# Attention with an MLP on one TensorE: each product with v split over two row halves, summed in two PSUM banks

## The chip, the core and the metric

One core of one Trainium2 chip runs the whole program. The metric is the device time of one execution in microseconds (us); lower is better.

## What is computed

`g * A(x) + (1 - g) * B(x)` for x of 2048 tokens by 576 features, in float32. A is softmax attention over all 2048 tokens with 32 heads of 18 features, B is a layer norm and an MLP of 4608 hidden units with a tanh GELU, and g a sigmoid gate per token.

```
q, k, v = qkv[0], qkv[1], qkv[2]
scores = jnp.einsum("bhqd,bhkd->bhqk", q, k) * Dh ** -0.5
p = _softmax(scores, axis=-1)
o = jnp.einsum("bhqk,bhkd->bhqd", p, v)
a = o.transpose(0, 2, 1, 3).reshape(B, S, D) @ wo
h = _gelu(jnp.einsum("bsd,df->bsf", layernorm(x), w1) + b1)
b = jnp.einsum("bsf,fd->bsd", h, w2) + b2
return g * a + (1 - g) * b
```

## The kernel before

The program has three stages: projections to q, k and v (to about 245 us of the profiled execution), a long loop in which attention and the MLP share TensorE (to about 2162 us), and the end of the output projection.

**Units.** The heads are taken in 16 pairs, and the queries in two halves of 1024: 32 units. A pair's two heads lie on the two row halves of the array, so a score product has 54 or 56 rows and 128 columns, and two of them run side by side. A unit has 16 steps (`kc`, 128 keys each) of two half steps (`qb`, 512 queries each). In a half step stand:

- `s2` (line 320): two score products, keys by queries. ScalarE takes the exponential of each (line 322) into a ring of buffers `p` and `ring`, which frees its PSUM bank.
- one round of `s1` (line 234): two score products for a later unit, queries by keys, of which VectorE takes the row maxima (line 236), which frees their banks.
- then either a stretch of the MLP (lines 611 and 751, written as pairs of products on the two row halves, `weave`), or of the output projection late in the loop (line 1353), or a visit to `pv`.

**The product with v.** `pv` (line 339) multiplies two or three finished steps (`room`) with v: for each step four products of 128 keys by 32 columns, one for each head and query block, which write partitions 0, 64, 32 and 96 of one bank and run in four column groups of the array. They accumulate over the 16 steps of the unit. The operands are float32 and not float32r as elsewhere, and the profile shows two matmul rows for each such product. At the end of the unit `o_store` copies the bank with VectorE (line 364) and stores it.

**Banks.** PSUM has eight banks. In the loop the MLP has two of its own (`ps_w`). The other six (`ps_x`, class `Earliest`) serve `s1`, `s2` and the open sum of a unit. Which bank a product takes is decided when the program is written: the one that a small model of the engines' clocks (`pe_t`, `act_t`, `dve_t`, `let_go`) believes to be free first. On the chip the product then waits for the engine that read the bank's former tile.

**Order.** The order on each engine is fixed by the code: `run_due` counts slots, and `defer(n, fn)` puts a piece of work n slots later. `s1_finish` turns a unit's maxima into two extra rows of q with such delays: `parts` on ScalarE, then `rows` on VectorE (lines 257 and 258) with eight small stores into `qa`. For unit 0 this lies ahead of the loop, where `looped[0]` is false.

Of the kernel before, what the change touches and what calls it, by code (L numbers as in the profile page):

```python
# [12 lines left out]
ALU = mybir.AluOpType  # L13
# [10 lines left out]
NT = S // P  # L24
# [39 lines left out]
def gated_mix_kernel(ctx: ExitStack, tc: tile.TileContext, x, wqkv, wo, w1, b1, w2, b2, gate_w, out):  # L64
    nc = tc.nc
# [34 lines left out]
    pe_t, act_t, dve_t = [0.0], [0.0], [0.0]  # L100
# [10 lines left out]
    taken = [0]  # L111
    ps_x = Earliest()
# [5 lines left out]
    def let_go(i, clock, ns):  # L118

        clock[0] = max(clock[0], pe_t[0] + DRAIN) + ns  # L120
        free_at[i] = clock[0]
# [5 lines left out]
    def psum(pool):  # L127
        return pool.tile([P, TB], F32, name="ps")
# [10 lines left out]
    def dma_r(queue, dst, src):  # L139

        queue.dma_start(dst.bitcast(F32), src)  # L141
# [5 lines left out]
    def defer(n, fn):  # L147
        later.append((slot[0] + n, fn))
# [13 lines left out]
    def run_due(ns=SLOT):  # L162

        slot[0] += 1
        now[0] += ns
        if chain and chain[0][0]():
            chain.pop(0)[1]()
        due = [f for t, f in timed if t <= now[0]]
        timed[:] = [(t, f) for t, f in timed if t > now[0]]
        for f in due:  # L170
            f()
        due = [f for s, f in later if s <= slot[0]]
        later[:] = [(s, f) for s, f in later if s > slot[0]]
        for f in due:
            f()
        k = 0
        while k < len(bg):
            if pool_end[0] - now[0] < bg[k][2] and slot[0] >= bg[k][0]():
                bg.pop(k)[1]()
                k = 0  # L180
            else:
                k += 1
# [12 lines left out]
    def unit(u):  # L195
        return UNITS[u]
# [44 lines left out]
    def s1_finish(u):  # L241

        m4 = M4.pop(u)
        nm = asm.tile([P, 2, 2, 8], F32, name="nm")
        nm2 = asm.tile([P, 2, 2, 8], F32, name="nm2")
        nmh = asm.tile([P, 2, 8], F32R, name="nmh")
        nc.vector.tensor_reduce(nm[:, 0], m4, axis=AX.X, op=ALU.max, negate=True)

        def parts():
            nc.scalar.activation(nmh, nm[:, 0], AF.Copy)  # L250
            nc.scalar.activation(nm[:, 1], nmh.bitcast(F32), AF.Copy, scale=-1.0)
            nc.scalar.activation(nm2[:, :, 0, :], nmh.bitcast(F32), AF.Copy)
            defer(2 if looped[0] else 8, rows)

        def rows():
            mr = asm.tile([P, 32], F32, name="mr", bufs=1)
            nc.vector.tensor_reduce(nm2[:, :, 1, :], nm.rearrange("p k a b -> p a b k"), axis=AX.X, op=ALU.add)
            nc.vector.transpose(mr, nm2.rearrange("p a b c -> p (a b c)"))
            qa = QA[u % 3]
            aside = slot[0] < ybusy[0]  # L260

            def store(h, k):
                r = 64 * h + 54
                c = 32 * k + 16 * h
                dst = qa[r:r + 2, :].rearrange("b (t k n) -> b t k n", k=4, n=32)[:, :, k, :]
                dma_r(nc.scalar if aside else nc.sync, dst, mr[c:c + 16, :])
            for n in range(8):
                if aside:
                    defer(1 + n, lambda n=n: store(*divmod(n, 4)))
                else:  # L270
                    store(*divmod(n, 4))
        defer(3 if looped[0] else 2, parts)

    RING = []

    def ring(n):
        return RING[n % 4 if n < NARROW else (n - NARROW) % 3]
# [6 lines left out]
    def flush():  # L284

        if held:
            for fn in waiting:
                fn()
            waiting.clear()
            tail = held.pop()  # L290
            tail()
# [45 lines left out]
    OB = {}  # L337

    def pv(n0, n1):

        flush()
        for c in range(n0, n1):
            u, k = divmod(c, NT)
            if k == 0:
                OB[u] = psum(ps_x), taken[0]
            v = VT[UNITS[u][0] % 2]
            for qb in range(2):
                for h in range(2):
                    r = 32 * (2 * h + qb)
                    nc.tensor.matmul(OB[u][0][r:r + 32, :], v[:, k, 19 * h:19 * h + 32], ring(c)[:, qb, h, :],  # L350
                                     start=(k == 0), stop=(k == NT - 1))
            pe_t[0] += 1040.0
            if k == NT - 1:
                o_store(u, *OB.pop(u))
        run_due(1040.0 * (n1 - n0))

    stored = []

    def o_store(u, ps, bank):

        pair, half = unit(u)
        oe = asm.tile([P, TB], F32, name="oe", bufs=1)
        dn = asm.tile([P, 16], F32, name="dn", bufs=1)
        nc.vector.tensor_copy(oe, ps)
        let_go(bank, dve_t, 620.0)
        cols = slice(2 * pair * DH, 2 * (pair + 1) * DH)
        nc.sync.dma_start(dn, oe[DH::32, :])
        for h in range(2):
            for qb in range(2):
                c = 32 * (2 * h + qb)  # L370
                d = (2 * pair + h) * DH
                q = half * HALF + qb * TB
                nc.sync.dma_start(ot_scr[0, d:d + DH, q:q + TB], oe[c:c + DH, :])

        def spread():
            nc.vector.reciprocal(dn, dn)
            nc.sync.dma_start(dn_scr[u], dn)
            defer(16 if u < NU - 3 else 4, wide)

        def wide():  # L380
            dst = ot_scr[1, cols, half * HALF:(half + 1) * HALF]
            nc.sync.dma_start(dst.rearrange("(h d) n -> h d n", d=DH), dn_scr[u][:, None, :].to_broadcast([2, DH, HALF]))
            stored.append(u)
        defer(24 if u < NU - 3 else 4, spread)
# [4 lines left out]
    looped = [False]  # L389
# [511 lines left out]
    with ExitStack() as a:  # L901
# [217 lines left out]
        for tb in range(NB):  # L1119
# [3 lines left out]
            for g, (fn, args) in enumerate(work):  # L1123
# [49 lines left out]
                if tb == 2 and g == 13:  # L1173
                    ps = psum(ps_x)
# [242 lines left out]
    for u in range(NU):  # L1417
        for kc in range(NT):
# [22 lines left out]
            if step - done[0] >= room[0] or room[0] == 3 and ended[0] and step > done[0]:  # L1441
                pv(done[0], step)
                done[0] = step
                piece[0] = 0
                ended[0] = 0
            else:
                fill(step)
            s2(u, kc, 1, loop_round(), 462.0)
            if not (room[0] == 3 and ended[0]):
                fill(step)  # L1450
    pv(done[0], NSTEP)
    while stream or later or timed or chain:
        filler(spent[0] + 1000.0)
# [26 lines left out]
```

## Time and profile before

| | us |
|---|---|
| median of three runs | 2215.01 (2215.0 to 2216.78) |
| profiled execution | 2215.03, of which the span from the first to the last instruction is 2213.1 |
| TensorE (PE) busy | 2196.4 |
| weight loads (PEld) busy | 1599.6 |
| VectorE (DVE) busy | 1644.7 |
| ScalarE (ACT) busy | 1436.3 |
| GpSimd (POOL) busy | 949.1 |
| loop, 260 to 2131 us: PE, DVE, ACT busy | 1869.1, 1448.6, 1312.8 |

The mean granted TensorE clock is 0.998. Matmuls overlap, so the busy time of PE says that something is always in flight, and not how close together products start; the start times in the timeline say that. Idle time of an engine is put down to whatever semaphore came last before it.

### The profile page before, as it was taken

What the parts mean: (1) busy time and instruction counts of PE and PEld (TensorE: products, weight loads), DVE (VectorE), ACT (ScalarE), POOL (GpSimd) and SP (SyncE); (2) the same over time, 40 slices, a digit from 0 to 9 for tenths busy, and PEclk for the clock granted to TensorE, in tenths of its full rate; (3) what the DMA queues carried; (4) which work ended last, traced back from release to release, by engine and by line L of the source; (5) the groups of instructions that cost most, each with busy time, mean ns of one, the idle gap of its engine ahead of it and who ended that gap; (6) DMA issues with size and microseconds to landing.
All of it is one profiled execution on the core that took longest, in us unless ns stands there. A gap on an engine that the chain in (4) does not pass through costs nothing. (4 is left out here: it accounts for less than half of the span.)

```text
span 2213.1 us, 51656 instructions
## 1 busy us (share of the span) xinstructions
PE 2196.4 (99%) x20569; PEld 1599.6 (72%) x20569; DVE 1644.7 (74%) x2887; ACT 1436.3 (65%) x2719; POOL 949.1 (43%) x936
## 2 busy tenths in 40 slices
PE   8999999999999999999999999999999999999999
PEld 7878777777767777677677676776677677777668
DVE  5675777777777777777777777777777777787844
ACT  4223677777776666666666666666766667666771
POOL 4002566666663444444445444444534444444420
PEclk9999999999999999999999999999999999999999
DMA  7755654536485423342273424243563333333355
GB/s 241 259 190 188 206 172 140 171 133 179 152 230 184 127 102 122 101 145 92 104 187 141 125 100 124 101 126 120 137 187 113 135 113 106 116 109 117 97 177 182
DMA packets 163414, 323.65 MB, mean 146 GB/s; under 512 B 59838, under 2 KB 86370, under 8 KB 152338
## 3 DMA queue, kind: packets, MB, share of 16 engines
q1 hardware_dynamic: 159462, 313.60, 44.4%
q10 hardware_dynamic: 3712, 6.75, 0.8%
q8 instruction: 162, 2.65, 0.5%
q14 instruction: 78, 0.64, 0.1%
HBM read 229.07 MB, written 95.16 MB: 147 GB/s over the span
## 5 line engine op out<-in xcount | busy, mean ns | idle before, releaser
L236 DVE TENSOR_REDUCE m<-ps 128x1 f32<-128x512 f32 x2048 | 1307.5, 684 | 392.0 <-PE ps L234 354.9
L322 ACT ACTIVATE p<-ps 128x512 f32<-128x512 f32 x1080 | 582.6, 596 | 283.4 <-PE ps L234 188.8
L322 ACT ACTIVATE ring<-ps 128x512 f32<-128x512 f32 x968 | 523.2, 596 | 259.5 <-PE ps L234 186.5
L320 PE MATMUL ps<-qa,ka 56*128 56x512 f32 x2048 | 685.9, 409 | 4.5 <-DMA qa<-mr 2.6
L234 PE MATMUL ps<-ka,qa 54*128 54x512 f32 x2048 | 625.6, 409 | 0.9 <-DVE big L968 0.7
L611 PE MATMUL ps<-big,w 64*128 64x512 f32 x3888 | 516.5, 392 | 0.1
L320 PEld LDWEIGHTS ps<-qa,ka 56*128 56x128 f32 x2048 | 358.4, 185 | 212.0 <-DVE m L236 130.8
L751 PE MATMUL ps<-w,hh 64*128 64x288 f32 x4352 | 491.2, 293 | 0.9 <-ACT z L636 0.8
L187 POOL TENSOR_SCALAR zz<-zz 128x512 f32<-128x512 f32 x272 | 169.2, 622 | 742.7 <-ACT zz L702 714.1
L751 PEld LDWEIGHTS ps<-w,hh 64*128 64x128 f32 x4352 | 418.1, 186 | 22.1 <-ACT z L636 1.2
L611 PEld LDWEIGHTS ps<-big,w 64*128 64x128 f32 x3888 | 380.6, 185 | 72.2 <-ACT vt L1066 0.3
L187 POOL TENSOR_TENSOR zz<-zz,z 128x512 f32<-128x512 f32 x280 | 361.8, 1293 | 35.9 <-ACT zz L705 9.8
L751 PE MATMUL ps<-w,hl 64*128 64x288 f32 x2176 | 340.7, 293 | 0.0
L234 PEld LDWEIGHTS ps<-ka,qa 54*128 54x128 f32 x2048 | 318.2, 186 | 23.1 <-issue 3.6
L350 PE MATMUL ps<-p,vt 128*32 128x512 f32 x2160 | 265.2, 598 | 0.0
L350 PE MATMUL ps<-ring,vt 128*32 128x512 f32 x1936 | 238.9, 598 | 0.0
L751 PEld LDWEIGHTS ps<-w,hl 64*128 64x128 f32 x2176 | 236.9, 186 | 0.0
L187 POOL TENSOR_TENSOR w<-x,w 128x576 fp32r<-128x576 f32 (+1 forms) x34 | 68.2, 2009 | 271.2 <-ACT w L490 206.6
L187 POOL TENSOR_TENSOR hl<-zz,hh 128x512 fp32r<-128x512 f32 x134 | 174.6, 1304 | 14.0 <-ACT hh L664 3.2
L350 PEld LDWEIGHTS ps<-p,vt 128*32 128x32 f32 x2160 | 57.9, 109 | 126.8 <-issue 124.2
L350 PEld LDWEIGHTS ps<-ring,vt 128*32 128x32 f32 x1936 | 52.3, 109 | 112.2 <-issue 111.2
L1037 PE MATMUL ps<-big,wqk 128*128 128x512 f32 x504 | 123.5, 400 | 0.0
(120 smaller groups left out, 1452.0 us busy)
## 6 DMA issues: line engine op xcount, KB each, us to landing
w<-w_scr SPq DMA_DIRECT2D x54, 1152.0 KB
w<-w_scr SPq DMA_DIRECT2D x108, 576.0 KB
w_scr<-w SPq DMA_DIRECT2D x18, 1152.0 KB
w_scr<-w SPq DMA_DIRECT2D x36, 576.0 KB
qa<-qk_scr SPq DMA_DIRECT2D x192, 72.0 KB
ka<-qk_scr SPq DMA_DIRECT2D x90, 144.0 KB
big<-y_scr SPq DMA_DIRECT2D x48, 256.0 KB
x<-in_B_w_dram SPq DMA_DIRECT2D x34, 288.0 KB
```

The costliest lines, as they stand in the source:

```text
L187: fn(*args, **kw)
L234: nc.tensor.matmul(ps, qa[r0:r0 + 54, t * P:(t + 1) * P], ka[r0:r0 + 54, kb * TB:(kb + 1) * TB], start=True, stop=True)
L236: nc.vector.tensor_reduce(M4[u][:, h, t, kb:kb + 1], ps, axis=AX.X, op=ALU.max)
L320: nc.tensor.matmul(ps, ka[r0:r0 + 56, kc * P:(kc + 1) * P], qa[r0:r0 + 56, qb * TB:(qb + 1) * TB], start=True, stop=True)
L322: nc.scalar.activation(ring(n)[:, qb, h], ps, AF.Exp, scale=SCALE)
L350: nc.tensor.matmul(OB[u][0][r:r + 32, :], v[:, k, 19 * h:19 * h + 32], ring(c)[:, qb, h, :], start=(k == 0), stop=(k == NT - 1))
L611: nc.tensor.matmul(ps[h], wt[w_][r, c, :], Y[s_][r, c, :], start=(k == 0), stop=(k == 26))
L751: mm = nc.tensor.matmul(ps[nn][:, :ND], h_[r, tok], w_[p_][r, cs[nn]], start=(k == 0 or bare and k == 3 * G), stop=(k == 6 * G - 1 or bare ...
L1037: nc.tensor.matmul(ps, w_[:, c, ms], big[:, s_, :], start=(k == 0), stop=(k == len(prods) - 1))
```

## The change

Each product with v is written as two, over keys 0 to 63 and 64 to 127 of the step. The tiles are 64 rows by 32 columns instead of 128 by 32. The upper and the lower half accumulate in two banks, so a unit's open sum holds two banks of the six. At the end of a unit VectorE copies the first bank and adds the second to the copy. One delay ahead of the loop goes from 8 slots to 4.

```diff
-            defer(2 if looped[0] else 8, rows)
+            defer(2 if looped[0] else 4, rows)
...
-                OB[u] = psum(ps_x), taken[0]
+                OB[u] = [(psum(ps_x), taken[0]) for _ in range(2)]
...
                 for h in range(2):
-                    r = 32 * (2 * h + qb)
-                    nc.tensor.matmul(OB[u][0][r:r + 32, :], v[:, k, 19 * h:19 * h + 32], ring(c)[:, qb, h, :],
-                                     start=(k == 0), stop=(k == NT - 1))
+                    for part in range(2):
+                        r = 32 * (2 * h + qb)
+                        keys = slice(64 * part, 64 * part + 64)
+                        nc.tensor.matmul(OB[u][part][0][r:r + 32, :], v[keys, k, 19 * h:19 * h + 32], ring(c)[keys, qb, h, :],
+                                         start=(k == 0), stop=(k == NT - 1))
             pe_t[0] += 1040.0
             if k == NT - 1:
-                o_store(u, *OB.pop(u))
+                o_store(u, OB.pop(u))
...
-    def o_store(u, ps, bank):
+    def o_store(u, parts):
...
-        nc.vector.tensor_copy(oe, ps)
-        let_go(bank, dve_t, 620.0)
+        nc.vector.tensor_copy(oe, parts[0][0])
+        let_go(parts[0][1], dve_t, 620.0)
+        nc.vector.scalar_tensor_tensor(oe, parts[1][0], 1.0, oe, op0=ALU.mult, op1=ALU.add)
+        let_go(parts[1][1], dve_t, 700.0)
```

Lines behind the edit move by four at most (751 becomes 755, 350 becomes 352). Apart from the added instructions and the one moved row step, every engine has its instructions in the same order as before; what differs is the bank of each score product, and so the engine it waits for.

TensorE at the half step that starts at 1005.42 us of the profile before, with a visit to `pv` behind it. In brackets stands the engine whose semaphore a product waits for. Before:

```order
L751 MATMUL ps<-w_13928,hh 128x288 x4
L751 MATMUL ps<-w_13928,hl 128x288 x2
L320 MATMUL ps<-qa_109,ka_112 128x512 [waits DVE_49]
L234 MATMUL ps<-ka_112,qa_110 128x512 [waits Activation_49]
L234 MATMUL ps<-ka_112,qa_110 128x512 [waits DVE_49]
L320 MATMUL ps<-qa_109,ka_112 128x512 [waits DVE_49]
L350 MATMUL ps<-ring_2274,vt_114 32x512 x4
L350 MATMUL ps<-ring_2282,vt_114 32x512 x4
```

And now:

```order
L755 MATMUL ps<-w_14711,hh 128x288 x4
L755 MATMUL ps<-w_14711,hl 128x288 x2
L320 MATMUL ps<-qa_109,ka_112 128x512 [waits Activation_49]
L234 MATMUL ps<-ka_112,qa_110 128x512 [waits DVE_49] x2
L320 MATMUL ps<-qa_109,ka_112 128x512 [waits DVE_49]
L352 MATMUL ps<-ring_2274,vt_114 32x512 x8
L352 MATMUL ps<-ring_2282,vt_114 32x512 x8
```

The eight products of the visit have become sixteen, and the four score products wait for other former tiles of their banks.

VectorE where a unit's sum is stored (`m` are the row maxima, `x` is the MLP's sum, `oe` the copy). Before:

```order
L721 SCALAR_TENSOR_TENSOR x<-ps,x 128x288 [waits PE_49] x2
L236 TENSOR_REDUCE m_3342<-ps 128x1 [waits PE_49] x2
L364 COPY oe<-ps 128x512 [waits PE_49]
L236 TENSOR_REDUCE m_3342<-ps 128x1 [waits PE_49] x6
L721 SCALAR_TENSOR_TENSOR x<-ps,x 128x288 [waits PE_49] x2
```

And now:

```order
L725 SCALAR_TENSOR_TENSOR x<-ps,x 128x288 [waits PE_49] x2
L236 TENSOR_REDUCE m_3387<-ps 128x1 [waits PE_49] x2
L366 COPY oe<-ps 128x512 [waits PE_49]
L368 SCALAR_TENSOR_TENSOR oe<-ps,oe 128x512 [waits DVE_49,PE_49]
L236 TENSOR_REDUCE m_3387<-ps 128x1 [waits PE_49] x6
L725 SCALAR_TENSOR_TENSOR x<-ps,x 128x288 [waits PE_49] x2
```

One add stands behind the copy, ahead of six reductions that were next in line.

## The prediction

> **What bounds the kernel now.** I read the page's totals and groups first, then the waits, then the timeline of single visits.
>
> ```profile
> span 2213.1 us, 51656 instructions
> PE 2196.4 (99%) x20569; PEld 1599.6 (72%) x20569; DVE 1644.7 (74%) x2887; ACT 1436.3 (65%) x2719; POOL 949.1 (43%) x936
> ...
> L236 DVE TENSOR_REDUCE m<-ps 128x1 f32<-128x512 f32 x2048 | 1307.5, 684 | 392.0 <-PE ps L234 354.9
> ...
> L320 PE MATMUL ps<-qa,ka 56*128 56x512 f32 x2048 | 685.9, 409 | 4.5 <-DMA qa<-mr 2.6
> L234 PE MATMUL ps<-ka,qa 54*128 54x512 f32 x2048 | 625.6, 409 | 0.9 <-DVE big L968 0.7
> ...
> L350 PE MATMUL ps<-p,vt 128*32 128x512 f32 x2160 | 265.2, 598 | 0.0
> L350 PE MATMUL ps<-ring,vt 128*32 128x512 f32 x1936 | 238.9, 598 | 0.0
> ```
>
> TensorE is the bound: 99% busy, and its two kinds of score product (L320 for the softmax, L234 for the maxima) sat idle for 4.5 and 0.9 us in all. So no score product waits today for a PSUM bank, and whatever makes TensorE wait, or stop waiting, shows in the time one to one. But busy is a modelled figure (products of 0.4 us start 0.23 us apart), so the edges between kinds of product must be read from start times. One visit to the product with v, from the timeline (start and length in us, engine, line, operation; PEld is the weight load; in brackets the engine's idle time before):
>
> ```profile
> 1200.62 0.62 PE L234 MATMUL ps<-ka,qa 54*128 54x512 f32 x2
> 1200.85 0.39 PE L320 MATMUL ps<-qa,ka 56*128 56x512 f32 x1
> 1201.17 0.16 PEld L350 LDWEIGHTS ps<-p,vt 128*32 128x32 f32 x8 [0.36 <-issue]
> 1201.17 1.07 PE L350 MATMUL ps<-p,vt 128*32 128x512 f32 x8
> 1201.62 0.13 PEld L350 LDWEIGHTS ps<-ring,vt 128*32 128x32 f32 x4 [0.30 <-issue]
> 1202.05 0.13 PEld L350 LDWEIGHTS ps<-ring,vt 128*32 128x32 f32 x4 [0.30 <-issue]
> 1202.48 0.13 PEld L350 LDWEIGHTS ps<-ring,vt 128*32 128x32 f32 x4 [0.30 <-issue]
> 1202.91 0.13 PEld L350 LDWEIGHTS ps<-ring,vt 128*32 128x32 f32 x4 [0.30 <-issue]
> 1203.88 0.18 PEld L320 LDWEIGHTS ps<-qa,ka 56*128 56x128 f32 x1 [0.84 <-issue]
> 1203.88 0.50 PE L320 MATMUL ps<-qa,ka 56*128 56x512 f32 x1
> ...
> 1204.22 0.40 PE L320 MATMUL ps<-qa,ka 56*128 56x512 f32 x1
> ```
>
> Four products start together, the next four 0.43 us later; the code's 2048 products are 4096 rows (2160 + 1936), two rows each, 1024 groups of four. The edges cost: into the visit 0.32 us between starts where score pairs take 0.23 (0.62 to 0.85), +0.09; the first group 0.45, +0.02; out of it, the last group (3.34, one pitch after 2.91) to 3.88 is 0.54, +0.11; then a pair of 0.34, +0.11, because no weights were loaded ahead. That is 0.33 us a visit. The visits are counted by the load's wait at the exit:
>
> ```profile
> PEld ps L320 <- DVE m L236: 130.8, 156, 0.8
> PEld ps L320 <- issue: 48.4, 59, 1.1
> PEld ps L320 <- DVE oe L364: 5.9, 7, 0.8
> ```
>
> 156 + 59 + 7 = 222 visits of 0.83 us idle each. VectorE is named only because its semaphore came last; it is the edge. 222 x 0.33 = 73 us lie in edges.
>
> **Part 1, products of 64 keys.** Each product becomes two, on the upper and the lower row half: 8192 rows in place of 4096. If both halves run together, as the L234 and L320 pairs of two row halves do, a group of eight takes the same 0.43 us and the streaming costs nothing. No row shows a product of 64 rows by 32 columns. The open point is the edge. Every change of shape in the trace drains; the other kind is seen late in the program:
>
> ```profile
> 2132.33 0.51 PE L320 MATMUL ps<-qa,ka 56*128 56x512 f32 x2
> ...
> 2132.76 1.09 PEld L1353 LDWEIGHTS ps<-big 128*128 128x128 f32 x8 [0.25 <-issue]
> 2132.76 1.32 PE L1353 MATMUL ps<-big 128*128 128x288 f32 x8
> ```
>
> Here columns stay at 128 and only the rows change; the next shape starts after 0.43 us, not 0.23. A change of columns alone, which is what remains after the edit, is in no row. Bounds: all edges stay (0) or all go (-73 us). I take 0, the nearer to rows in which no change of shape was free. The Trainium skill, TensorEngine Tiling (Array Packing), Key Properties, says that changing the tiling mode, not only the tile, drains the engine, and lists 64 x 32 and 64 x 128 as different modes; by it the sum below is 2354 us, and were it untrue here 2277; no run here shows that case yet.
>
> Eight weight loads and products must be issued at an edge in place of four. Within a visit the starts of a group spread over about 0.02 us; eight spread over twice that or more, some 0.03 us more a visit: +7 us. Sustained, 16 instructions per 0.43 us is one per 27 ns. The densest quoted stretch:
>
> ```profile
> 1204.46 0.43 PE L751 MATMUL ps<-w,hh 64*128 64x288 f32 x4
> 1204.73 0.30 PE L751 MATMUL ps<-w,hl 64*128 64x288 f32 x2
> 1204.86 0.43 PE L751 MATMUL ps<-w,hh 64*128 64x288 f32 x4
> ```
>
> Six products and six loads in 0.40 us, 33 ns each, and that is the array's pace, not shown to be the sequencer's. I take 0; the other end, 33 ns, is a rival.
>
> **Part 2, the second bank.** In the loop six banks serve the score products and the open sum of the unit; two more belong to the MLP. The sum now holds two, which leaves four. What four would do is read from the rows today:
>
> ```profile
> 1003.59 2.52 DVE L236 TENSOR_REDUCE m<-ps 128x1 f32<-128x512 f32 x4 [0.86 <-PE ps L234]
> ...
> 1004.39 0.41 PE L234 MATMUL ps<-ka,qa 54*128 54x512 f32 x2
> ...
> 1005.42 0.40 PE L320 MATMUL ps<-qa,ka 56*128 56x512 f32 x1
> 1005.42 0.39 PE L234 MATMUL ps<-ka,qa 54*128 54x512 f32 x1
> ...
> 1005.66 0.40 PE L320 MATMUL ps<-qa,ka 56*128 56x512 f32 x1
> 1005.66 0.40 PE L234 MATMUL ps<-ka,qa 54*128 54x512 f32 x1
> 1005.92 1.08 ACT L322 ACTIVATE p<-ps 128x512 f32<-128x512 f32 x2 [1.28 <-PE ps L320]
> ```
>
> At 1005.66 five score tiles are alive: the second maximum of 1004.39 (the fourth reduction of the 2.52 us run frees it at 1006.11), the two of 1005.42, and the two that start. With the sum that is six banks, all there are. With four, the last product waits until 1006.11, 0.45 us. The order shows the changed program's last L320 there waiting for VectorE. I made this count for all 3582 score products that start while a sum is open: 327 have a fifth tile alive. The first and last:
>
> ```profile
> 325.54 0.40 PE L320 MATMUL ps<-qa,ka 56*128 56x512 f32 x1
> ```
>
> ```profile
> 2128.96 0.39 PE L320 MATMUL ps<-qa,ka 56*128 56x512 f32 x1
> ```
>
> From each start to the next release is 0.34 us on average (0.05 of it from a release to the start that it lets go, the least that these rows show), 111 us in all. Waits shorten later ones, since ScalarE and VectorE catch up; carrying each delay forward through their rows leaves 100 us. A product that waits also loads its weights only then, 0.11 us as at the exit: about 300 x 0.11 = 33 us. I take 133; the low end is 75 (waits a quarter shorter, loads half hidden), the high end 111 + 36 = 147.
>
> **Part 3, VectorE's add.** Nearest rows:
>
> ```profile
> L635 DVE TENSOR_SCALAR z<-ps,b1t 128x512 f32<-128x512 f32 x71 | 53.3, 750 | 10.8 <-PE ps L611 10.8
> ...
> L364 DVE COPY oe<-ps 128x512 f32<-128x512 f32 x32 | 22.1, 690 | 7.3 <-PE ps L350 7.3
> ```
>
> 32 adds of 0.69 to 0.75 us are 24 us on an engine that is 74% busy. Queued behind an add are the reductions that free banks; those waits (the first products of a unit need two free banks too) are within the 100. Only the last unit's add lies on the path: +1.
>
> **Part 4, the shorter delay** (8 slots to 4, outside the loop) takes unit 0's row step on VectorE past four reductions, about two rounds; it can end at most the 2.6 us that L320 waited for qa<-mr. -2.
>
> **Sum.** The profiled execution took 2215.03 us (span 2213.1), the median is 2215.01, so one base: 2215 + 0 (edges) + 7 + 133 + 1 - 2 = 2354 us. Its own range: 2215 + 0 + 75 + 1 - 2 = 2289 with the low ends, 2215 + 11 + 147 + 1 = 2374 with the high ones (a spread of 0.05 us a visit, no gain at the start).
>
> **Rivals.** *The edges go.* If only the row split matters to the array, score products load ahead across both edges: -73 and no spread; the banks cost the same 133, a little more since starts come closer (+3). 2215 - 73 + 136 - 1 = 2277 us, 2240 to 2300. For it: after the edit rows are always split. Against: the row above.
>
> *Faster: the edges go and a blocked product stops only its own row half.* It decides when the banks cost under 74 us, 0.23 us per short start where I have 0.34 + 0.11. With half the price, 68 us, it gives 2215 - 73 + 68 - 1 = 2209; with a third, 2186, which I take. Against it, the longest stop:
>
> ```profile
> 2097.94 0.18 PEld L320 LDWEIGHTS ps<-qa,ka 56*128 56x128 f32 x1 [1.97 <-DVE x L721]
> ...
> 2097.94 0.40 PE L751 MATMUL ps<-w,hh 64*128 64x288 f32 x1
> ```
>
> The other half's product, L751, starts only when the blocked L320 does: both halves stop.
>
> *Issue becomes the bound.* 16 instructions at 33 ns are 0.53 us a group, +0.10 x 1024 = 102 us on top: 2456.
>
> *The halves do not run together*, so that the split does not do what it says: 1024 x 0.43 = 440 us more, 2794.
>
> **Chances.** Edges stay 0.56; edges go 0.24; faster rival 0.11, of which 0.02 within 0.2%; issue 0.06; halves apart 0.03. 0.2% (4.4 us) is about what a measurement of this kernel tells from no change. Faster 0.09, same 0.02, slower 0.89. The first two cases hold 0.80: 2240 to 2375.
>
> **What would show it.** In the changed profile: groups of eight 0.43 us apart; the load's idle before L320 still about 0.83 us at each of 222 exits (edges stay) or gone; some 300 new waits of L320 and L234 for DVE m and ACT p, together about 100 us; VectorE some 24 us busier. Wrong would be a group pitch off 0.43 us, or bank waits under 70 us.

## The result and the profile after

The changed kernel takes 2336.69 us (median of four runs, 2334.4 to 2338.61) against 2215.27 us (2215.0 to 2216.78): a ratio of 1.0546 (95% interval 1.0528 to 1.0564), 121 us slower. The profiled execution has a span of 2332.6 us. The page, in the lines that answer to those of before:

```profile
span 2332.6 us, 59780 instructions
PE 2300.3 (99%) x24665; PEld 1673.0 (72%) x24665; DVE 1673.6 (72%) x2919; ACT 1457.6 (62%) x2719; POOL 946.3 (41%) x936
...
L320 PE MATMUL ps<-qa,ka 56*128 56x512 f32 x2048 | 764.3, 422 | 19.8 <-DVE m L236 4.1
L234 PE MATMUL ps<-ka,qa 54*128 54x512 f32 x2048 | 614.0, 411 | 1.4 <-DVE big L972 0.7
...
L320 PEld LDWEIGHTS ps<-qa,ka 56*128 56x128 f32 x2048 | 358.2, 184 | 308.7 <-issue 166.9
...
L352 PE MATMUL ps<-p,vt 64*32 64x512 f32 x4320 | 272.0, 594 | 0.1
L352 PE MATMUL ps<-ring,vt 64*32 64x512 f32 x3872 | 241.9, 594 | 0.0
```

TensorE is still 99% busy, 104 us more than before, and the products with v have the same modelled time in twice as many rows. PE's own idle column explains little: L320 went from 4.5 to 19.8 us. While one score product is blocked, an earlier one is still in flight by the profile, and the engine counts as busy. The wait shows in the weight load, which has to stand still first. The same group of before reads:

```profile
L320 PEld LDWEIGHTS ps<-qa,ka 56*128 56x128 f32 x2048 | 358.4, 185 | 212.0 <-DVE m L236 130.8
```

The load's idle time grew from 212.0 to 308.7 us, by 96.7. Added up over the trace, 188.6 us of it stand at the exits from `pv` in both kernels; the rest grew from 23.4 to 120.1 us. The waits of the changed kernel say for what (us in total, times, longest):

```profile
PEld ps L320 <- issue: 166.9, 200, 0.8
PEld ps L320 <- DVE m L236: 78.6, 179, 1.0
PEld ps L320 <- ACT ring L322: 21.9, 72, 0.8
PEld ps L320 <- ACT p L322: 19.5, 69, 0.3
PEld ps L320 <- ACT zz L706: 5.9, 7, 0.8
```

The row "issue" has 200 idle times of 0.83 us: these are exits from `pv`, most of which were put down to VectorE before. The five rows hold 527 idle stretches. Before, the rows of 130.8, 48.4 and 5.9 us quoted in the prediction and the row for ACT p held 232:

```profile
PEld ps L320 <- ACT p L322: 2.5, 10, 0.5
```

So there are about 295 new ones, which stand for a reader of a bank. They could also come from the program's fixed choice of banks, if a product stood for one bank while another was free. The trace says no: of the 308 stops outside the exits (idle times over 0.15 us), 273 with 92.7 us of idle time start within 0.12 us of the end of a reader, with four score tiles alive, which is every bank that is left; the other 35 hold 17 us. Before, with a fifth bank, 2 stops came with all banks full. One of them, in a half step with a visit to `pv` behind it, as in the prediction's count (start and length in us; idle time of the engine before it in brackets):

```profile
1004.77 0.40 PE L320 MATMUL ps<-qa,ka 56*128 56x512 f32 x1
1004.81 0.68 DVE L236 TENSOR_REDUCE m<-ps 128x1 f32<-128x512 f32 x1
...
1004.99 0.45 PE L234 MATMUL ps<-ka,qa 54*128 54x512 f32 x2
...
1005.54 0.18 PEld L320 LDWEIGHTS ps<-qa,ka 56*128 56x128 f32 x1 [0.41 <-DVE m L236]
1005.54 0.50 PE L320 MATMUL ps<-qa,ka 56*128 56x512 f32 x1
1005.97 0.18 PEld L352 LDWEIGHTS ps<-ring,vt 64*32 64x32 f32 x16 [0.25 <-issue]
```

The last L320 of the half step starts 0.05 us after the reduction at 1004.81 has ended (1005.49), 0.55 us after the product ahead of it and not 0.23. Its weights are loaded only at 1005.54, and so the visit behind it starts 0.43 us later, where the visit of before came 0.32 us after an unblocked product. Both parts of the price are here: the wait, and 0.11 us of a load that nothing hides.

A whole visit in the weight loads of the changed kernel:

```profile
1269.83 0.18 PEld L352 LDWEIGHTS ps<-p,vt 64*32 64x32 f32 x16 [0.24 <-issue]
1270.29 0.15 PEld L352 LDWEIGHTS ps<-p,vt 64*32 64x32 f32 x8 [0.28 <-issue]
1270.71 0.15 PEld L352 LDWEIGHTS ps<-p,vt 64*32 64x32 f32 x8 [0.28 <-issue]
1271.71 0.18 PEld L320 LDWEIGHTS ps<-qa,ka 56*128 56x128 f32 x1 [0.84 <-issue]
```

Eight products in a group where there were four: the second starts 0.46 us after the first (0.45 before), and from there they are 0.42 to 0.43 us apart as before. The last group starts one pitch after 1270.71, at 1271.14, and the exit to 1271.71 is 0.57 us (0.54 before). The load's idle time at the exit is 0.84 us, unchanged.

### The profile page after: what moved, and what is told of

Read it like the earlier page. It is cut to its first block, busy times and chain, and to the rows that moved or that the text cites. A ratio compares the mean times of both kernels' runs of the same rounds, so it can differ in the third digit from the quotient of the medians.

```text
span 2332.6 us, 59780 instructions
## 1 busy us (share of the span) xinstructions
PE 2300.3 (99%) x24665; PEld 1673.0 (72%) x24665; DVE 1673.6 (72%) x2919; ACT 1457.6 (62%) x2719; POOL 946.3 (41%) x936
## 5 line engine op out<-in xcount | busy, mean ns | idle before, releaser
L320 PE MATMUL ps<-qa,ka 56*128 56x512 f32 x2048 | 764.3, 422 | 19.8 <-DVE m L236 4.1
L234 PE MATMUL ps<-ka,qa 54*128 54x512 f32 x2048 | 614.0, 411 | 1.4 <-DVE big L972 0.7
L320 PEld LDWEIGHTS ps<-qa,ka 56*128 56x128 f32 x2048 | 358.2, 184 | 308.7 <-issue 166.9
L755 PE MATMUL ps<-w,hh 64*128 64x288 f32 x4352 | 543.9, 295 | 0.9 <-ACT z L640 0.8
L755 PEld LDWEIGHTS ps<-w,hh 64*128 64x128 f32 x4352 | 449.7, 186 | 15.1 <-ACT z L640 1.2
L615 PEld LDWEIGHTS ps<-big,w 64*128 64x128 f32 x3888 | 406.6, 185 | 52.8 <-ACT vt L1070 0.3
L755 PE MATMUL ps<-w,hl 64*128 64x288 f32 x2176 | 401.4, 292 | 0.0
L234 PEld LDWEIGHTS ps<-ka,qa 54*128 54x128 f32 x2048 | 327.3, 185 | 24.3 <-ACT p L322 4.2
L755 PEld LDWEIGHTS ps<-w,hl 64*128 64x128 f32 x2176 | 302.1, 185 | 0.0
L352 PE MATMUL ps<-p,vt 64*32 64x512 f32 x4320 | 272.0, 594 | 0.1
L352 PE MATMUL ps<-ring,vt 64*32 64x512 f32 x3872 | 241.9, 594 | 0.0
L352 PEld LDWEIGHTS ps<-p,vt 64*32 64x32 f32 x4320 | 73.0, 106 | 112.9 <-issue 101.8
L352 PEld LDWEIGHTS ps<-ring,vt 64*32 64x32 f32 x3872 | 61.1, 106 | 101.0 <-issue 100.2
```

What stands on the lines that cost most here:

```text
L234: nc.tensor.matmul(ps, qa[r0:r0 + 54, t * P:(t + 1) * P], ka[r0:r0 + 54, kb * TB:(kb + 1) * TB], start=True, stop=True)
L320: nc.tensor.matmul(ps, ka[r0:r0 + 56, kc * P:(kc + 1) * P], qa[r0:r0 + 56, qb * TB:(qb + 1) * TB], start=True, stop=True)
L352: nc.tensor.matmul(OB[u][part][0][r:r + 32, :], v[keys, k, 19 * h:19 * h + 32], ring(c)[keys, qb, h, :], start=(k == 0), stop=(k == NT - 1))
L615: nc.tensor.matmul(ps[h], wt[w_][r, c, :], Y[s_][r, c, :], start=(k == 0), stop=(k == 26))
L755: mm = nc.tensor.matmul(ps[nn][:, :ND], h_[r, tok], w_[p_][r, cs[nn]], start=(k == 0 or bare and k == 3 * G), stop=(k == 6 * G - 1 or bare ...
```

## The experiments

Theory: the 121 us are the bank that the second sum takes from the score products (about 115), and the edges of a visit stay, a little dearer with eight tiles. First rival: the banks cost little and the 121 us lie in the products with v themselves (issue, edges). Second rival: the add on VectorE holds up the reductions behind it.

**1. The bank alone.** The kernel before, with its products with v unchanged; each open sum keeps a second bank that nothing writes.

```diff
-                OB[u] = psum(ps_x), taken[0]
+                OB[u] = psum(ps_x), taken[0], []
+                for _ in range(1):
+                    psum(ps_x)
+                    OB[u][2].append(taken[0])
...
-    def o_store(u, ps, bank):
+    def o_store(u, ps, bank, held_):
...
         let_go(bank, dve_t, 620.0)
+        for i in held_:
+            let_go(i, dve_t, 700.0)
```

> The kernel before with one thing added: each unit's open sum keeps a second bank of the six out of use, in which nothing is written. Products with v, edges and VectorE's work are those of before. Theory (the second bank is the cost): score products wait for banks as in the changed kernel, some 300 waits, about 115 us with the weight loads behind them, so 2330 us (2315 to 2345) and L320's weight load idle for about 95 us more than before. Rival (the 64-row products or their edges are the cost): no more than 2225 us.

Measured: 2329.27 us (2328.93 to 2329.35) beside 2216.14, ratio 1.0513 (1.0497 to 1.0529): 113 us for a bank in which no product is ever written. The groups and the waits of this run:

```profile
L320 PEld LDWEIGHTS ps<-qa,ka 56*128 56x128 f32 x2048 | 360.0, 185 | 306.5 <-issue 150.5
```

```profile
PEld ps L320 <- issue: 150.5, 180, 1.1
PEld ps L320 <- DVE m L236: 75.5, 166, 1.0
PEld ps L320 <- ACT ring L322: 34.5, 87, 0.8
PEld ps L320 <- ACT p L322: 22.0, 71, 0.8
PEld ps L320 <- ACT zz L707: 5.9, 7, 0.8
```

306.5 - 212.0 = 94.5 us more idle, and 511 stretches against 232: nearly the picture of the changed kernel, without its products. By the start and end times, at most four score tiles are alive while a sum is open, where the kernel before has up to five; so the bank is out of use. The bank is 113 of the 121 us, and the first rival keeps 8.

**2. Two banks.** The same with `range(2)`, which leaves three banks for the score products.

> As the kernel with one bank held, but with two held, so that three of six banks are left for score products. Theory: carrying the waits forward through the rows of the kernel before gives 177 us, 2392 us (2365 to 2440), with about twice the number of waits. Rival (a bank more or less does not matter): the same as with one bank held.

Measured: 2943.35 us (2940.57 to 2945.53), ratio 1.3284 (1.3265 to 1.3304). The forecast of 2392 was wrong by far: the second bank costs 614 us, more than five times the first. The groups, the waits and the timeline show what the forecast left out:

```profile
L320 PEld LDWEIGHTS ps<-qa,ka 56*128 56x128 f32 x2048 | 375.0, 185 | 840.0 <-DVE m L236 268.7
```

```profile
PEld ps L320 <- ACT p L322: 252.1, 362, 1.3
PEld ps L320 <- ACT ring L322: 225.0, 317, 1.2
```

```profile
1201.07 0.49 PE L320 MATMUL ps<-qa,ka 56*128 56x512 f32 x1 [0.48 <-ACT p L322]
...
1202.34 0.39 PE L320 MATMUL ps<-qa,ka 56*128 56x512 f32 x1
...
1202.56 0.40 PE L234 MATMUL ps<-ka,qa 54*128 54x512 f32 x2
1202.79 0.60 ACT L322 ACTIVATE p<-ps 128x512 f32<-128x512 f32 x1 [0.59 <-PE ps L320]
...
1203.44 0.18 PEld L320 LDWEIGHTS ps<-qa,ka 56*128 56x128 f32 x1 [0.91 <-ACT p L322]
```

A half step has four score tiles. With three banks its fourth, the L320 of 1203.44, must wait for the exponential of its first, which begins at 1202.79 and ends at 1203.39. The wait for exponentials is the larger part (252.1 + 225.0 = 477 us of the load's idle time, against 268.7 put down to reductions, some of them exits). A stop of more than 0.15 us outside the exits stands in 810 of the 1024 half steps, where the kernel before has one in 27; spread over all, 727 us are 0.71 us a half step. The count behind the forecast shifted the starts of the trace before and took each bank's reader to have begun already; that holds for four banks, where the fourth tile needs the tile of an earlier half step, and not for three. That this is the whole of the 551 us between forecast and result is argued, not shown.

**3. Same columns.** The changed kernel, with the products with v as tiles of 64 rows by 128 columns, streaming 128 queries in place of 512, so that a tile takes one row half and all columns, as a score product does. The attention output is another computation here.

```diff
-                        r = 32 * (2 * h + qb)
+                        c0 = min(VW * k + 19 * h, NT * VW - P)
+                        r = P * (2 * h + qb)
...
-                        nc.tensor.matmul(OB[u][part][0][r:r + 32, :], v[keys, k, 19 * h:19 * h + 32], ring(c)[keys, qb, h, :],
-                                         start=(k == 0), stop=(k == NT - 1))
+                        nc.tensor.matmul(OB[u][part][0][:, r:r + P], v.rearrange("p k e -> p (k e)")[keys, c0:c0 + P], ring(c)[keys, qb, h, 0:P],
+                                         start=(k == 0 and qb + h == 0), stop=(k == NT - 1 and qb + h == 2))
```

> The changed kernel with products with v in the shape of the score products, 64 rows by 128 columns, each streaming 128 of its 512 queries, so that the streaming of a step stays about 0.86 us (0.85 to 0.95); 128 neighbouring columns of v are taken as weights, so the attention output is not the reference's. float32 in two rows each stays. Theory (the edge belongs to the change of column shape): the load's idle of 0.8 us at the exits is gone, a score pair follows at the pitch of its neighbours, and the time falls by the edges, 80 us, less 0 to 45 us of slower streaming: 2257 to 2302 us. Rival (the edge belongs to float32 products or to the visit itself): the edges stay, 2335 to 2385 us.

Measured: 2256.79 us (2254.9 to 2258.04), ratio 1.0185 (1.017 to 1.0201), 80 us under the changed kernel. The groups, the waits and one visit:

```profile
L320 PEld LDWEIGHTS ps<-qa,ka 56*128 56x128 f32 x2048 | 376.0, 185 | 142.5 <-DVE m L236 89.0
...
L353 PE MATMUL ps<-p,vt 64*128 64x128 f32 x4320 | 315.2, 275 | 0.4
```

```profile
PEld ps L320 <- DVE m L236: 89.0, 308, 1.0
PEld ps L320 <- ACT ring L322: 20.3, 70, 0.6
PEld ps L320 <- ACT p L322: 18.9, 67, 0.6
```

```profile
1210.57 0.18 PEld L320 LDWEIGHTS ps<-qa,ka 56*128 56x128 f32 x1 [0.16 <-DVE m L236]
1210.57 1.87 PEld L353 LDWEIGHTS ps<-ring,vt 64*128 64x128 f32 x30
1210.68 0.40 PE L320 MATMUL ps<-qa,ka 56*128 56x512 f32 x1
1210.68 1.96 PE L353 MATMUL ps<-ring,vt 64*128 64x128 f32 x30
...
1212.47 0.27 PE L353 MATMUL ps<-p,vt 64*128 64x128 f32 x1
...
1212.58 0.27 PE L353 MATMUL ps<-p,vt 64*128 64x128 f32 x1
```

The first product with v starts with the score product beside it, at 1210.68, and the row of 200 exits ("issue", 166.9 us) is gone. The bank waits are still there. So the edge hangs on the column shape, 32 against 128, and not on the split of the rows or on float32, which both stay. The streams are shorter here too (128 against 512), which the run doesn't hold apart from the shape. The 80 us agree in size with the 73 + 7 that the prediction put at the edges, but are no clean price: pairs 0.11 us apart (1212.47, 1212.58) make 0.88 us of the 8 pairs of a step where two groups take 0.86, and score products now run beside products with v.

**4. Without the add.** The changed kernel less VectorE's add; the output lacks the lower half's sums.

```diff
-        nc.vector.scalar_tensor_tensor(oe, parts[1][0], 1.0, oe, op0=ALU.mult, op1=ALU.add)
```

> The changed kernel without VectorE's 32 adds: the sums over the lower row half are left out of the output. Theory (the adds lie beside other work, their delays of later reductions are a small part of the bank waits): 1 to 6 us faster than the changed kernel, 2331 to 2336 us. Rival (the adds hold up the reductions that free banks, all of it on the path): 24 us or more faster, 2312 us or less.

Measured: 2334.19 us (2330.79 to 2335.12), ratio 1.0533 (1.0517 to 1.0548). VectorE's 32 adds are gone, and 21.2 us of its busy time with them (1652.4 against 1673.6), and the time falls by 2.5 us, which the intervals don't tell from nothing. The second rival falls.

**5. The old delay.** The changed kernel with 8 slots again.

```diff
-            defer(2 if looped[0] else 4, rows)
+            defer(2 if looped[0] else 8, rows)
```

> The changed kernel with the delay ahead of the loop back at 8 slots. Theory: 0 to 2.6 us slower than the changed kernel, 2337 to 2340 us, with L320's first wait for qa<-mr back. Rival (the shorter delay moves the whole loop's pattern): more than 4 us either way.

Measured: 2338.12 us (2337.22 to 2338.83), ratio 1.0553 (1.0536 to 1.0571): 1.4 us above the changed kernel, as expected in sign and size, and inside the scatter. L320's wait for qa<-mr is back in the main: 2.2 us of idle time on the matmul, against 1.2 in the changed kernel and 2.6 before.

**6 and 7. Banks to spare.** Both kernels, with the maxima taken over the first 512 keys alone; the products and reductions of the other three quarters are left out, so that fewer tiles are alive at once: in the kernel before, 353 score products start with five or more score tiles alive, here 51.

```diff
+            if kb:
+                return
...
-        nc.vector.tensor_reduce(nm[:, 0], m4, axis=AX.X, op=ALU.max, negate=True)
+        nc.vector.tensor_reduce(nm[:, 0], m4[:, :, :, 0:1], axis=AX.X, op=ALU.max, negate=True)
```

> The kernel before with three quarters of the maxima left out: the row maxima are taken over the first 512 keys alone, so 1536 of the 2048 L234 products and their reductions are gone, and fewer score tiles are alive at once. Alone it says little; it is the base of the next kernel. About 180 us (768 pairs of 0.23) less work on TensorE: 2035 us (2000 to 2080).

> The changed kernel with the same three quarters of the maxima left out. Theory (the cost is the shortage of banks): with few tiles alive the second bank costs little, and what is left of the difference to the kernel before with the same omission is the wider exit of 222 visits, 5 us, and some last waits: 5 to 30 us in place of 121. Rival (64-row products or their edges cost by themselves): about 120 us again.

Measured: 2049.96 us (2048.93 to 2051.58) from the kernel before, 2073.82 us (2071.11 to 2076.59) from the changed one. The change costs 24 us here, not 121. The load's groups, first of the kernel before with a quarter of the maxima, then of the changed one:

```profile
L322 PEld LDWEIGHTS ps<-qa,ka 56*128 56x128 f32 x2048 | 263.2, 185 | 221.5 <-issue 186.5
```

```profile
L322 PEld LDWEIGHTS ps<-qa,ka 56*128 56x128 f32 x2048 | 263.0, 185 | 229.4 <-issue 141.1
```

Its idle time grows by 7.9 us and not by 96.7. With few tiles alive, the second bank costs little. The two profiled executions lie 26 us apart, and the start times divide this: the visits with their exits are 8 us longer in sum (471.5 to 479.4), their entries 5 us (74.2 to 79.1), and the products for the maxima start 13 us later behind the product ahead of them (47.3 to 59.9), where their weight load's idle time grows from 6.7 to 15.9 us. The first 8 us are the spread at the edges. The other 18 fit waits for banks, but no run here holds them apart from the rest.

## Why the prediction was right, point by point

The forecast was 2354 us by the likeliest case, "edges stay"; the time is 2337, and the mechanism is that case.

**Edges: 0 forecast, none gone.** The exits kept their 0.84 us of load idle, and the products after them start 0.57 and not 0.23 us after the last group. A change between tiles of 64 x 32 and 64 x 128 drained (0.57 us), and 64 x 128 after 64 x 128 did not (experiment 3). The Trainium skill, TensorEngine Tiling (Array Packing), Key Properties, states that a change of tiling mode drains the engine; the trace agrees. The rivals in which the edges go, 2277 and 2186 us, fall with the 0.57 us. The second of them also needed a blocked product to stop only its own row half, and the changed kernel shows that it stops both:

```profile
1274.12 0.60 PE L234 MATMUL ps<-ka,qa 54*128 54x512 f32 x2
1274.65 0.50 PE L320 MATMUL ps<-qa,ka 56*128 56x512 f32 x1
1274.66 0.63 PE L755 MATMUL ps<-w,hh 64*128 64x288 f32 x3
```

L755 has banks of its own and starts with the blocked L320. It is so each time: 131 of the 308 stopped L320 have an L755 next, and it starts 3 to 7 ns after the L320.

**Streaming: 0 forecast, 0 found.** The pitch of a group is 0.43 us with eight products as with four. The rivals "issue" (2456) and "halves apart" (2794) fall.

**Spread at the edges: 7 forecast, 8 found.** Added up over the start times of all visits (226 of them; the three rows of the load's waits in the prediction hold 222), the time from a visit's first product to the product after its last is 471.2 us before, 471.3 in experiment 1 and 479.3 in the changed kernel: 8 us, 0.036 a visit. The changed kernel less experiment 1 is 2336.7 - 2329.3 = 7.4 us, which holds the spread, the add and the delay (forecast 7 + 1 - 2 = 6).

**Banks: 133 forecast, 113 found.** This is the term that was mis-sized: it is 20 us over, where the whole misses by 17. Experiment 1 measures the 113, and the changed kernel leaves the same when the spread is taken off (121 - 8). The number of waits was about right: some 300 forecast, 295 new idle stretches in the changed kernel, 279 in experiment 1. The price of one was less: 133 / 300 = 0.44 us forecast, 113 / 295 = 0.38 found in the changed kernel, 113 / 279 = 0.41 in experiment 1.

The load's idle time grew by 96.7 us where waits of 100 and late loads of 33 were forecast beside one another; part of the waits is shorter, or part of the loads still hidden. One piece can be told apart: the starts at the entry of the visits, where a late load shows by itself, lie 73.6 us apart in sum before and 86.3 after, +13 us. For waits ahead of the MLP the rows give the load's idle time, and not the wait apart from what it makes late, so the split of the other 100 us stays open. They are all at score products: the time from the start ahead of a product to its own start grows by 94 us in sum for L320 and by 6 for L234, and for the other products outside the visits by none (-1). 113 lies within the term's bounds, 75 to 147.

Two readings behind this term don't hold as they stand. The prediction took the 4.5 us of idle time in PE's column of L320 to say that no score product waited for a bank before. It was right by luck: the same column has 19.8 us in the changed kernel, where some 100 us are waits. The load's 23.4 us outside the exits bear it out. And the row of 2128.96, shown as the last start with a fifth tile alive, is none: two score tiles are alive there, and the last such start is at 2087.90. By the rows, 310 of the 3688 score products that start while a sum is open have five alive, not 327 of 3582; to the next release, with the 0.05 us behind it, they add up to 110 us in place of 111, so the term stays.

**Add and delay: +1 and -2 forecast.** Experiments 4 and 5 give +2.5 and -1.4, neither told from zero. VectorE is 28.9 us busier, against 24 forecast; the adds are 21.2 of it, and the other 7.7 are in experiment 1 too, which has no add.

**What the forecast did not see** is how near the edge four banks are. The same count, asked for three banks, was wrong by 551 us (experiment 2). By the timeline there, it is good only while a blocked tile waits for a reader that runs already.

## What to carry to other kernels

Before a PSUM bank is given to something else, count in the trace how many tiles are alive at each product's start: each start with one too many pays the time to the next release and the weight load behind it, and when one round needs more tiles than there are banks, most rounds wait for a reader of their own (810 of 1024 here). A busy share of 99% doesn't show such waits; the idle time of the weight load does. The drain between two kinds of product went here only where the tile shape became the same, and splitting the rows of one of them did not bring that about.

## What the runs showed of the hardware

Sixteen instructions of TensorE (eight loads, eight products) went through in 0.43 us, 27 ns each, over four groups in a row and without loss; the densest stretch quoted of before had 33 ns. The drain did not care that eight small tiles ran in place of four: 0.57 us against 0.54. And one bank less cost 113 us, two cost 727: the step from five to four banks is a nuisance here, that from four to three puts a wait into most half steps, and TensorE's busy share falls from 99% to 87%.
